# Ten output stores cut into 64, 49 and 15 rows, to share the rows unevenly among the DMA engines

## The chip, the core and the metric

The kernel runs on one NeuronCore of a Trainium2 chip. The metric is device time in microseconds, the median of several executions. A verdict of faster or slower needs 2%; the ratios come with a 95% interval.

## The reference

Grouped attention with four query positions, and its gradients:

```
B, Hq, Hkv, Sq, Sk, D = 32, 32, 4, 4, 2048, 128      # bf16
scores = einsum("bhqd,bhkd->bhqk", q, repeat(k, 8)) * D ** -0.5
out    = einsum("bhqk,bhkd->bhqd", softmax(scores), repeat(v, 8))
# returned: out, and the gradients of q, k, v for a given grad_out
```

K and V (with q and grad_out) are read once, and dK and dV (with out and dq) written once: 136.3 MB each way. There is little arithmetic for each byte.

## The kernel before

The host code lays K and V out as two arrays each, so that one batch is four loads and four stores of 128 rows with 8,192 or 8,448 bytes in a row (the longer rows carry q, grad_out, out and dq as well). Twenty buffers ("slots") hold loaded and finished rows. A precomputed string, `PLAN`, gives the order of all units of work and the slot of each; `emit` turns it into instructions. Every load and store is issued by SyncE, in the order of the plan.

```python
SLOTS, E_TILES, DS_TILES = 20, 2, 2
...
        if name in ("LK", "LV"):                      # load 128 rows into a slot
            x = slots[int(u.where, 36)]
            ...
            nc.sync.dma_start(out=x[:, 0:n], in_=src)
...
        elif name in ("DVe", "DKe"):                  # PSUM to the output slot
            i, g = divmod(i, 2)
            copy = nc.scalar.copy if u.where == "A" else nc.vector.tensor_copy
            copy(out=t[name[:2], "out", g][:, 2 * QW * i:2 * QW * i + 2 * QW], in_=t[name[:2], i, g])
        elif name in ("SV", "SK"):                    # store a slot
            half, g = divmod(i, 2)
            n = LONG if g else ROW
            w = (slice(0, n), slice(0, ROW // 2), slice(ROW // 2, n))[half]
            nc.sync.dma_start(out=(dv_r if name == "SV" else dk_r)[g][b][:, w], in_=t["D" + name[1], "out", g][:, w])
```

In the built program the DMA issues take eight semaphores in turn. From the ninth on, an issue waits until the DMA eight places before it has landed, so at most eight DMAs are in flight.

## Time and profile before

| | before |
|---|---|
| median | 677.4 us |
| data moved | 272.65 MB |
| DMA data queue busy, share of 16 engines | 98.4% |
| PE, ACT, DVE busy | 92%, 85%, 83% |

The table of windows of the kernel before follows. Each row is a stretch of 100 us: its length, busy us of PE, PE weight loads, DVE, ACT and GpSimd with counts, the granted clock, the busy share of the DMA engines, and GB/s.

```profile
core 0: us, PE busy (x) PEld busy (x) DVE busy (x) ACT busy (x) POOL busy (x), PEclk, DMA share, GB/s
...
100.00:200.00 100.00, 97.42 (x1399) 64.74 (x1399) 89.56 (x115) 92.90 (x135) 7.18 (x18) 1.00 1.01 422
200.00:300.00 100.00, 94.75 (x1418) 63.60 (x1417) 87.91 (x111) 89.89 (x131) 5.98 (x15) 1.00 1.01 424
300.00:400.00 100.00, 91.36 (x1308) 61.71 (x1296) 83.33 (x104) 85.50 (x124) 4.78 (x12) 0.97 1.01 414
400.00:500.00 100.00, 91.05 (x1322) 61.87 (x1320) 82.79 (x106) 84.94 (x124) 5.99 (x15) 0.97 1.01 411
500.00:600.00 100.00, 91.08 (x1292) 61.16 (x1294) 84.82 (x109) 88.60 (x128) 6.20 (x16) 1.00 1.01 405
```

The DMA engines look busy all the time, yet the rate falls after 300 us. The first five lines of the waits of SyncE's queue of DMA issues tell what an issue waited for (line, releaser, us in total, times, longest). L229 is the loads, L324 the stores.

```profile
SPq L229 <- DMA out_dram<-row: 226.4, 46, 8.2
SPq L324 <- DVE row L319: 79.3, 19, 14.9
SPq L324 <- ACT row L319: 71.5, 37, 9.2
SPq L324 <- DMA out_dram<-row: 57.8, 33, 2.3
SPq L229 <- DMA row<-in_v_dram: 32.4, 16, 2.8
```

Issues wait mostly for older DMAs to land. The landings of one DMA can be told apart: the trace has the semaphore updates, and a whole DMA makes 16, one for each DMA engine. Sorted, and counted back from the last one, they read as follows (medians over the whole transfers around each time):

```
us from start    first landing   8th     15th    16th (last)
100                 -3.2         -2.8    -0.2     0
200                 -6.2         -4.3    -0.4     0
300                -10.0         -5.4    -2.5     0
400                -10.6         -7.8    -4.5     0
```

The engines drift apart, because each works through its own share at its own pace. A DMA is complete only when the slowest has landed. From 300 us on the spread stays near 11 us: the fast engines now keep pace with the slowest. This is where the rate falls.

### The profile page before, as it was taken

To read this page: it belongs to the slowest core of one execution; us is meant where nothing else is said; L and a number is where in the kernel's file an instruction comes from. 1 tells how busy PE (TensorE), PEld (TensorE's weight loads), DVE (VectorE), ACT (ScalarE), POOL (GpSimd) and SP (SyncE) were. 2 spreads that over 40 slices of the span, in tenths; PEclk is the share of its full clock that TensorE was granted. 3 is DMA by queue.
4 is the path that set the end of the run, shared out by engine and by line. 5 is a ranking of instruction groups with operands and counts; after the bars stand their busy time and mean duration, and the time that the engine had idled before them with its cause. 6 is when DMAs were issued, how large, how long until landed. Compare 5 with 4: busy or idle time off the path is not lost.

```text
span 677.2 us, 20820 instructions
## 1 busy us (share of the span) xinstructions
PE 620.9 (92%) x8788; PEld 416.3 (61%) x8788; DVE 560.2 (83%) x712; ACT 578.8 (85%) x826; POOL 39.0 (6%) x102
## 2 busy tenths in 40 slices
PE   8899999999999999889999899989899889988995
PEld 7565666666666665656656565666666556655652
DVE  3678988989888888888878888879788888887886
ACT  5878999999999998888888889879888888997876
POOL 0000000000000000000000000000000000000000
PEclk9997999999999999999989999989989999998988
DMA  9999999999999999999999999999999999999698
GB/s 368 399 418 403 389 424 420 415 424 425 425 422 426 422 424 425 424 423 408 423 414 403 414 403 416 413 419 397 418 404 416 414 395 405 398 390 388 219 421 327
DMA packets 37533, 273.97 MB, mean 405 GB/s; under 512 B 4160, under 2 KB 4160, under 8 KB 5184
## 3 DMA queue, kind: packets, MB, share of 16 engines
q1 hardware_dynamic: 37440, 272.65, 98.4%
q8 instruction: 69, 1.13, 0.6%
q14 instruction: 24, 0.20, 0.1%
HBM read 136.31 MB, written 136.31 MB: 403 GB/s over the span
## 4 chain that ended last, share of the span: by engine, by line
DMA 61%; PE 25%; ACT 7%; DVE 3%; issue 2%; SPq 1%; DVEq 0%; ACTq 0%
DMA out_dram<-row 49%; PE psum L244 14%; DMA row<-in_k_dram 10%; ACT row L319 5%; PE psum L313 5%; PE psum L291 3%; PE psum L258 3%; DMA row<-in_v_dram 2%; SPq L229 1%; DVE row L319 1%; ACT vt_sb L212 1%; DVE vt_sb L214 1%; DVE dt_sb L214 1%; ACT kt_sb L212 0%; DVE e_sb L263 0%
## 5 line engine op out<-in xcount | busy, mean ns | idle before, releaser
L319 ACT CAST row<-psum 128x1024 bf16<-128x1024 f32 x302 | 297.3, 1026 | 46.7 <-PE psum L313 23.5
L244 PE MATMUL psum<-ident,row 128*128 128x128 f32 x2048 | 300.0, 286 | 19.8 <-DVE vt_sb L214 5.0
L319 DVE CAST row<-psum 128x1024 bf16<-128x1024 f32 x210 | 252.7, 1217 | 41.6 <-PE psum L313 20.6
L244 PEld LDWEIGHTS psum<-ident,row 128*128 128x128 f32 x2048 | 226.9, 144 | 94.4 <-ACT row L319 30.5
L212 ACT COPY kt_sb<-psum 128x512 f32<-128x512 f32 x181 | 106.0, 596 | 22.4 <-PE psum L244 18.2
L212 ACT COPY vt_sb<-psum 128x512 f32<-128x512 f32 x181 | 102.4, 605 | 8.6 <-PE psum L244 8.5
L306 DVE SCALAR_TENSOR_TENSOR ds_sb<-psum,delta,e_sb 128x1024 bf16<-128x1024 f32 x64 | 81.9, 1279 | 25.5 <-PE psum L258 24.6
L313 PE MATMUL psum<-e_sb,dop_sb 32*128 32x512 bf16 x512 | 79.0, 389 | 19.5 <-ACT row L319 18.8
L313 PE MATMUL psum<-ds_sb,qp_sb 32*128 32x512 bf16 x512 | 80.5, 390 | 4.5 <-DVE row L319 1.7
L263 DVE TENSOR_SCALAR_CACHE_REDUCE e_sb<-psum 128x2048 bf16<-128x2048 f32 x32 | 73.3, 2291 | 11.1 <-PE psum L258 11.0
L267 ACT ACTIVATE e_sb<-psum,m 128x2048 bf16<-128x2048 f32 x32 | 63.9, 1998 | 0.7 <-DVE e_sb L263 0.7
L214 DVE COPY kt_sb<-psum 128x1024 bf16<-128x1024 bf16 x75 | 51.0, 682 | 11.1 <-PE psum L244 10.5
L313 PEld LDWEIGHTS <-dop_sb 32*128 32x128 bf16 x512 | 24.3, 92 | 52.5 <-issue 44.7
L214 DVE COPY vt_sb<-psum 128x1024 bf16<-128x1024 bf16 x75 | 49.0, 683 | 5.0 <-PE psum L244 4.7
L274 POOL TENSOR_SCALAR dop_sb<-row,rinv 128x128 bf16<-128x128 bf16 x32 | 19.4, 605 | 576.9 <-DVE rinv L271 435.8
L313 PEld LDWEIGHTS <-qp_sb 32*128 32x128 bf16 x512 | 21.6, 91 | 46.6 <-issue 43.2
L291 PE MATMUL psum<-row,dt_sb 128*32 128x128 bf16 x2048 | 41.0, 222 | 0.3 <-DVE row L319 0.3
L291 PEld LDWEIGHTS <-dt_sb 128*32 128x32 bf16 x2048 | 33.4, 96 | 12.7 <-issue 7.9
L244 PE MATMUL psum<-ident,ds_sb 128*128 128x128 f32 x256 | 40.2, 281 | 1.0 <-ACT row L319 1.0
L258 PE MATMUL psum<-vt_sb,qdt_sb 128*32 128x512 bf16 x512 | 39.8, 385 | 0.9
L291 PEld LDWEIGHTS <-et_sb 128*32 128x32 bf16 x2048 | 30.7, 96 | 11.0 <-ACT et_sb L212 8.8
L258 PEld LDWEIGHTS <-qdt_sb 128*32 128x32 bf16 x1024 | 21.7, 95 | 25.1 <-issue 17.0
(34 smaller groups left out, 351.3 us busy)
## 6 DMA issues: line engine op xcount, KB each, us to landing
row<-in_k_dram SPq DMA_DIRECT2D x64, 1056.0 KB, 17.5
row<-in_v_dram SPq DMA_DIRECT2D x64, 1024.0 KB, 15.5
out_dram<-row SPq DMA_DIRECT2D x62, 1056.0 KB, 19.4
out_dram<-row SPq DMA_DIRECT2D x62, 1024.0 KB, 20.0
out_dram<-row SPq DMA_DIRECT2D x6, 512.0 KB, 4.4
out_dram<-row SPq DMA_DIRECT2D x2, 544.0 KB, 4.6
```

What stands on the lines that cost most here:

```text
L212: nc.scalar.copy(out=out.bitcast(FP32), in_=in_)
L214: nc.vector.tensor_copy(out=out, in_=in_.bitcast(BF16))
L229: nc.sync.dma_start(out=x[:, 0:n], in_=src)
L244: nc.tensor.transpose(out=ps[:, P * j:P * j + P], in_=src[:, 4 * half + j, :], identity=ident32[:])
L258: nc.tensor.matmul(out[r, QW * w:QW * w + QW], lhsT=t["qdt"][:, P * side + 32 * h:P * side + 32 * h + 32], rhs=t[x, NH * i + h][:, QW * w: ...
L263: nc.vector.tensor_scalar(out=t["e"][:], in0=t["S"], scalar1=-scale, scalar2=None, op0=ALU.mult, op1=ALU.min, accum_out=t["m"][:])
L267: nc.scalar.activation(out=t["e"][:], in_=t["S"], func=ACT.Exp, bias=t["m"][:], scale=scale, accum_out=t["l"][:])
L274: nc.gpsimd.tensor_scalar(out=t["dop"][:], in0=t["go"], scalar1=t["rinv"][:], scalar2=None, op0=ALU.mult)
L291: nc.tensor.matmul(t[name][r, :], lhsT=left[:, j, r, odd], rhs=right[:, 4 * i + j, :, odd], start=(i == 0 and c == 0), stop=(i == 1 and c ...
L306: nc.vector.scalar_tensor_tensor(out=t["ds"][:, w], in0=t["DP", i], scalar=t["dl"][:], in1=t["e"][:, w], op0=ALU.subtract, op1=ALU.mult)
L313: nc.tensor.matmul(acc[:, QW * (h % 2):QW * (h % 2) + QW], lhsT=t[still][rows[h], :], rhs=t[moving][rows[h], QW * i:QW * i + QW], start=Tr ...
L319: copy(out=t[name[:2], "out", g][:, 2 * QW * i:2 * QW * i + 2 * QW], in_=t[name[:2], i, g])
```

## The change

The intent is to move rows from engines that fall behind to engines that run ahead. In batches 1, 4, 7, ... the first dV store goes out as three DMAs of 64, 49 and 15 rows, which use 16, 7 and 15 engines. The plan was made anew for it: the whole `PLAN` string differs and is cut here.

```diff
+PARTS = slice(0, 64), slice(64, 113), slice(113, 128)
+
...
-    "a000e400e011f4A0f0A0e522f5D0e133f1A0a110c000d0A0e214f2D0e345f3A0e726f7D0e607f6A0i040i1-0b120g600g211h6A0h2A0g322"
+    "a000e400e511f4A0e122f1A0e033f0A0f5D0a110c000e644f6A0e215f2D0e326e737d0A0f7D0f3A0i040i1-0D0b120g200h2A0g311h3A0"
... (the rest of PLAN)
-            nc.sync.dma_start(out=(dv_r if name == "SV" else dk_r)[g][b][:, w], in_=t["D" + name[1], "out", g][:, w])
+            dst, src = (dv_r if name == "SV" else dk_r)[g][b][:, w], t["D" + name[1], "out", g][:, w]
+            for p in PARTS if name == "SV" and i == 0 and b % 3 == 1 else (slice(0, P),):
+                nc.sync.dma_start(out=dst[p], in_=src[p])
```

The condition holds in ten batches. The last batch, no. 31, stores by halves of the columns under other part numbers and is never split by rows.

## The prediction

> **What bounds it now.** The DMA engines. By the table of DMA queues the data queue is busy 98.4% of 16 engines' span; PE is 92% busy. Yet the rate falls: by the table of windows 422 to 424 GB/s at 100 to 300 us, 414, 411 and 405 in the next three hundreds. The waits of the DMA-issuing queue name stores: loads (L229) wait 226.4 us for `out_dram<-row`: a load needs a slot that a store has left on all 16 engines.
>
> The trace's semaphore updates tell why. Each DMA counts 16 landings, one per engine. Sorted, they split into seven early, eight middle, one late, and drift apart: first to last 3 us at 100 us, 7.8 at 254, 11 at 307. Then the spread stays at 10 to 11: all slots wait for the late engine, and the early engines starve. Between 150 and 300 us the interval between full DMAs is 2.49 us for the early ranks, 2.54 for the middle, 2.57 for the last; between 350 and 580 us it is 2.62 for all. So starving costs more than the late engine's own pace. Instruction fetches (69 packets of 16 KB, about 0.95 us each) are part of the unevenness.
>
> **What the change does.** The Trainium skill, "DMA: Bandwidth & Descriptors", section on why a DMA increments its semaphore by 16, says that such a DMA uses the largest divisor of its rows up to 16, on the lowest-numbered engines; its section on latency calls engines 7 and 15 usually slower. Then a split store gives engines 0-6 4+7+1=12 rows, 7-14 4+1=5, 15 4, instead of 8 each. The 7/8/1 grouping of the landings agrees; that no. 15 is the late one the trace doesn't tell (engines aren't named). A row of 8 KB takes 309 ns. In 11 batches (1, 4, ... 31): +13.6 us for seven engines, -10.2 for eight, -13.6 for one. Bytes stay. Added: 22 issues of about 0.35 us on a queue that mostly waits, and 242 semaphore packets of 9 ns.
>
> **Worth.** Per batch of eight DMAs (estimate from the intervals): early 19.91+0.41=20.32 us, middle 20.32-0.31=20.01, late 20.55-0.41=20.14. The slowest is now 20.3, where the kernel ran 20.5 until 300 us and 20.9 after. All of it is critical. 256 full DMAs at 2.54 = 650; plus start, 9 us (90 landed by 240 us); plus end, 4; plus stalls of the new plan. Before, the dip at 600 to 640 us (310 GB/s; the queue waits 16.4 us for L299 with loads behind it) cost about 10. I allow 3 us. PE's 19.4 us a batch leaves it 95% busy: little slack.
>
> Predicted: 666 us, 658 to 675. Faster by over 2% 0.36, within 2% 0.61, slower 0.03.
>
> **Signs.** Data queue: same 272.65 MB, 37,682 packets. Spread of the landings under 6 us at 300 us, no saturation near 11. Windows from 300 to 600 us at 418 GB/s or more. Loads' wait for stores well under 226 us; stores land in under 19.4 us. Early ranks no longer early: the middle eight lead by up to 12 us at the end.
>
> **What would make it wrong.** Engines 0-6 read 49 rows that other engines otherwise read: if rows collide in SBUF, 309 ns grows (seven rows, 11 times: 24 us if doubled). The middle group runs ahead until slots bind again. The compute chain, with PE at 95%, binds before DMA does. The new end has a dip of its own.

## The result, and the profile after

The changed kernel takes 708.4 us (707.1 to 709.5, four runs), against 677.7 us for the kernel before in the same rounds. The ratio is 1.0455, interval 1.0428 to 1.0482: slower by 4.5%. A ratio here is the mean time of one kernel's runs over that of the other's of the same rounds, so not quite the ratio of the medians quoted. Executions over 1.5% slower than the fastest of the same kernel are left out of the means.

The table of windows of the kernel after, same columns:

```profile
core 0: us, PE busy (x) PEld busy (x) DVE busy (x) ACT busy (x) POOL busy (x), PEclk, DMA share, GB/s
...
100.00:200.00 100.00, 91.41 (x1280) 61.41 (x1278) 83.88 (x110) 85.44 (x120) 4.79 (x12) 0.98 1.01 415
200.00:300.00 100.00, 91.70 (x1331) 61.85 (x1334) 83.39 (x110) 84.48 (x119) 5.98 (x15) 0.95 1.00 406
300.00:400.00 100.00, 88.85 (x1230) 59.80 (x1223) 79.36 (x103) 79.01 (x112) 5.98 (x15) 0.93 0.97 379
400.00:500.00 100.00, 90.56 (x1231) 60.14 (x1230) 80.14 (x104) 81.43 (x114) 4.79 (x12) 0.90 0.99 388
500.00:600.00 100.00, 86.93 (x1231) 58.64 (x1231) 79.09 (x103) 79.31 (x111) 5.98 (x15) 0.95 0.99 380
```

The rate was meant to stay at 418 GB/s or more after 300 us. It is 379 to 388, and the fall begins 100 us earlier. The low rate from 500 us on may in part be a dip that comes with the new order of units: e1_plan_only, an experiment below with that order and whole stores, has a lower rate there and still takes only 679.2 us.

```profile
500.00:600.00 100.00, 90.16 (x1240) 59.31 (x1239) 79.63 (x105) 81.31 (x115) 6.00 (x15) 0.93 0.93 366
```

The waits of SyncE's queue after (L231 loads, L328 stores):

```profile
SPq L231 <- DMA out_dram<-row: 176.9, 54, 5.5
SPq L328 <- DVE row L321: 100.4, 31, 10.8
SPq L231 <- DMA row<-in_v_dram: 64.7, 33, 2.8
SPq L328 <- DMA out_dram<-row: 64.6, 35, 3.2
SPq L328 <- ACT row L321: 36.8, 15, 6.6
```

The wait of loads for stores went down, from 226.4 to 176.9 us, as predicted, and the kernel is slower all the same. Loads wait more for V loads instead (64.7 us, 32.4 before), which no slot explains: these are waits for one of the eight semaphores. But both shifts come with the new order of units and not with the split, since e1_plan_only shows them too:

```profile
SPq L231 <- DMA out_dram<-row: 172.5, 44, 5.5
SPq L231 <- DMA row<-in_v_dram: 79.7, 41, 2.1
```

So these waits don't explain the loss, and a smaller total in one row of them is not a gain.

The data queue, before and then after (packets, MB, busy share):

```profile
q1 hardware_dynamic: 37440, 272.65, 98.4%
```

```profile
q1 hardware_dynamic: 37660, 272.65, 96.9%
```

Each engine that takes part in a DMA posts one semaphore packet. The three pieces together make 16+7+15=38 instead of 16, so 22 more, ten times: 220, and 37,660 is exactly that. The engine counts of the diff's intent are right. The Trainium skill, "DMA: Bandwidth & Descriptors", section "Why a DMA increments its semaphore by 16 and not by 1", gives the rule behind them (the largest divisor of the row count up to 16) and says that the issuing sequencer adds what is missing to 16 itself. The trace agrees on that too: a 49-row piece has eight updates, seven landings and one at the time of its issue.

The spread of the landings after, in the same form as before:

```
us from start    first landing   8th     15th    16th (last)
100                 -5.4         -3.2    -0.3     0
200                -13.5        -11.5    -5.8     0
300                -12.8        -12.0   -10.4     0
400                -14.7        -14.6   -13.2     0
```

It grows about twice as fast, and in the end fifteen engines stand close together, with one alone 10 to 13 us behind. The pieces of a single split store say which kind of engine that is. These are the landings of the ones issued at 366.1, 368.3 and 370.9 us, in us before the last landing of each:

```
64 rows, last landing 387.2:  -14.5 -14.3 -14.3 -14.2 -14.0 -13.8 -13.7 -13.4 -13.3 -13.2 -13.0 -12.7 -12.7 -12.7 -12.2  0
49 rows, last landing 389.5:  -14.6 -14.5 -14.4 -13.9 -13.9 -13.2   0
15 rows, last landing 389.8:  -16.2 -16.2 -15.7 -15.4 -15.0 -15.0 -15.0 -14.6 -14.5 -14.4 -14.4 -13.9 -13.9 -13.2   0
```

The late engine is one of the seven that take the 49 rows. It gets 4+7+1=12 rows of a split store instead of 8. The change loads the engine that it was to relieve.

### The profile page after: what moved, and what is told of

Read it like the earlier page. It is cut to its first block, busy times and chain, and to the rows that moved or that the text cites. A ratio compares the mean times of both kernels' runs of the same rounds, so it can differ in the third digit from the quotient of the medians.

```text
span 705.2 us, 20835 instructions
## 1 busy us (share of the span) xinstructions
PE 629.6 (89%) x8788; PEld 420.8 (60%) x8788; DVE 565.7 (80%) x734; ACT 576.8 (82%) x804; POOL 39.1 (6%) x102
## 3 DMA queue, kind: packets, MB, share of 16 engines
q1 hardware_dynamic: 37660, 272.65, 96.9%
## 4 chain that ended last, share of the span: by engine, by line
DMA 56%; PE 29%; ACT 6%; DVE 4%; issue 3%; SPq 0%; ACTq 0%; DVEq 0%
DMA out_dram<-row 30%; DMA row<-in_v_dram 22%; PE psum L246 17%; PE psum L315 6%; ACT row L321 5%; DMA row<-in_k_dram 5%; PE psum L260 3%; PE psum L293 3%; DVE row L321 1%; DVE dt_sb L216 1%; DVE vt_sb L216 1%; DVE ds_sb L308 1%; DVE e_sb L265 0%; ACT e_sb L269 0%; SPq L231 0%
## 5 line engine op out<-in xcount | busy, mean ns | idle before, releaser
L321 ACT CAST row<-psum 128x1024 bf16<-128x1024 f32 x324 | 319.7, 1024 | 73.0 <-DMA out_dram<-row 43.5
L246 PEld LDWEIGHTS psum<-ident,row 128*128 128x128 f32 x2048 | 234.3, 147 | 83.3 <-ACT row L321 38.0
L321 DVE CAST row<-psum 128x1024 bf16<-128x1024 f32 x188 | 228.5, 1219 | 46.1 <-DMA out_dram<-row 39.8
L214 ACT COPY kt_sb<-psum 128x512 f32<-128x512 f32 x183 | 106.3, 597 | 16.2 <-PE psum L246 15.7
L315 PE MATMUL psum<-e_sb,dop_sb 32*128 32x512 bf16 x512 | 84.3, 412 | 35.0 <-ACT row L321 34.9
L216 DVE COPY vt_sb<-psum 128x1024 bf16<-128x1024 bf16 x124 | 82.4, 685 | 15.8 <-PE psum L246 14.2
L214 ACT COPY vt_sb<-psum 128x512 f32<-128x512 f32 x132 | 74.9, 597 | 10.5 <-PE psum L246 10.3
L315 PEld LDWEIGHTS <-dop_sb 32*128 32x128 bf16 x512 | 21.8, 92 | 65.2 <-issue 54.6
L260 PE MATMUL psum<-vt_sb,qdt_sb 128*32 128x512 bf16 x512 | 43.1, 414 | 1.0 <-ACT row L321 0.4
L260 PE MATMUL psum<-kt_sb,qdt_sb 128*32 128x512 bf16 x512 | 35.1, 382 | 3.9 <-DVE row L321 3.7
```

The lines of the kernel that those rows point to most:

```text
L214: nc.scalar.copy(out=out.bitcast(FP32), in_=in_)
L216: nc.vector.tensor_copy(out=out, in_=in_.bitcast(BF16))
L246: nc.tensor.transpose(out=ps[:, P * j:P * j + P], in_=src[:, 4 * half + j, :], identity=ident32[:])
L260: nc.tensor.matmul(out[r, QW * w:QW * w + QW], lhsT=t["qdt"][:, P * side + 32 * h:P * side + 32 * h + 32], rhs=t[x, NH * i + h][:, QW * w: ...
L315: nc.tensor.matmul(acc[:, QW * (h % 2):QW * (h % 2) + QW], lhsT=t[still][rows[h], :], rhs=t[moving][rows[h], QW * i:QW * i + QW], start=Tr ...
```

## The experiments

Three theories were tested. A: the rows of the one late engine set the time, and the split gives it more. B: the pieces cost the time as such, because each takes one of eight semaphores. C: the new order of units is worse by itself. "The late engine" is written as no. 4 where the probe below is presupposed.

### The parts alone, and a split that moves no rows

e1_plan_only is the changed kernel with whole stores; e2_split_only is the kernel before with the split; e3_three_even is the changed kernel with three pieces that leave every engine its eight rows.

```diff
 # e1_plan_only, against the changed kernel
-PARTS = slice(0, 64), slice(64, 113), slice(113, 128)
+PARTS = slice(0, 128),
 # e3_three_even, against the changed kernel
-PARTS = slice(0, 64), slice(64, 113), slice(113, 128)
+PARTS = slice(0, 48), slice(48, 96), slice(96, 128)
 # e2_split_only, against the kernel before: PARTS and the loop over it as in the change, PLAN untouched
```

> The new order of units, every store whole. Theory A (one engine that is already late is among the seven that take the 49 rows, so the split gives it 12 rows instead of 8) and theory B (the split takes three of the eight DMA semaphores, so less work is in flight) both put the loss into the split: 668 to 682 us, first-to-last spread of landings as before, saturating near 10 to 11 us. Theory C (the new order of units is worse by itself): 700 us or more.

> The old order of units, with the split in the same ten stores. A and B: 695 to 715 us, with the spread of landings saturating near 13 us well before 250 us, and the rate below 400 GB/s after it. C: within 1% of 677.7 us.

> The new order, the same ten stores in three pieces of 48, 48 and 32 rows: each engine gets 3+3+2=8 rows as in a whole store, but three semaphores are taken as in the change. A: as e1_plan_only within 1%. B: as the changed kernel, 700 us or more. If both act, in between.

| kernel | order | pieces | rows of the late engine | median us | ratio to before (interval) |
|---|---|---|---|---|---|
| before | old | whole | 8 | 677.5 | 1 |
| e1_plan_only | new | whole | 8 | 679.2 | 1.0015 (0.9987 to 1.0043) |
| e3_three_even | new | 48, 48, 32 | 8 | 682.8 | 1.0063 (1.0025 to 1.0101) |
| e2_split_only | old | 64, 49, 15 | 12 | 693.2 | 1.0220 (1.0189 to 1.0252) |
| changed kernel | new | 64, 49, 15 | 12 | 708.4 | 1.0455 (1.0428 to 1.0482) |

C falls: the new order alone costs nothing that is clear of noise. B explains about 3.6 us, the difference of e3_three_even and e1_plan_only; their intervals overlap, so that it is hardly clear of noise itself. Moving the rows costs the rest, some 25 us in the new order. In the old order the split costs 15.7 us: 693.2 us is just below the 695 to 715 expected. The spread of landings in e2_split_only reached 11 us at 200 us instead of 300, but stayed at 11 to 12 where 13 was expected, and its rate was 401 to 411 GB/s between 100 and 500 us and 389 only after that, where less than 400 was expected. The spread in e1_plan_only missed too: it went on to 13 us at 400 us instead of 10 to 11, but the 15th landing came only 7.8 us before the last there, against 13.2 in the changed kernel.

### Which engine is late

The section of the skill quoted above says that a DMA issued by SyncE runs on the lowest-numbered engines. If so, pieces of 1, 2, 3, ... rows ask one more engine each time.

```diff
 # e4_probe, against the kernel before
+PIECES = {10: (1, 2, 3, 4, 5, 6, 7, 100), 13: (8, 9, 10, 11, 12, 13, 14, 51), 16: (15, 98, 15)}
-            nc.sync.dma_start(out=(dv_r if name == "SV" else dk_r)[g][b][:, w], in_=t["D" + name[1], "out", g][:, w])
+            dst, src = (dv_r if name == "SV" else dk_r)[g][b][:, w], t["D" + name[1], "out", g][:, w]
+            at = 0
+            for n in PIECES.get(b, (P,)) if name == "SV" and i == 0 else (P,):
+                nc.sync.dma_start(out=dst[at:at + n], in_=src[at:at + n])
+                at += n
```

> The old order; the first dV store of batch 10 goes in pieces of 1, 2, 3, 4, 5, 6, 7 and 100 rows, that of batch 13 in 8 to 14 and 51 rows, that of batch 16 in 15, 98 and 15. If a piece of n rows uses the n lowest engines, the landings of the pieces name each engine's lag. The prediction's reading (the late engine is no. 15): no piece below 16 engines lands with the late one; every piece lands 3 to 9 us before the whole store beside it. Theory A: from some n below 8 on, the last landing of a piece comes with the late landing of the whole stores, 4 us or more after its other landings. The time itself may be 1 to 2% longer by the many pieces.

Landing times in us from the start, of the load just before the pieces and of the first five pieces in batch 10:

```
whole:    242.2 242.3 242.3 242.5 243.1 244.5 245.7 245.8 246.3 246.4 246.7 247.1 247.5 247.9 248.9 251.1
1 row :   242.6
2 rows:   242.9 244.8
3 rows:   243.2 243.4 245.1
4 rows:   243.5 243.7 245.4 246.1
5 rows:   244.6 244.7 245.7 246.4 251.4
```

No piece on up to four engines lands with the late engine. The first on five engines does: 251.4 us, just after the whole load's 251.1. So the fifth engine is the late one, no. 4 if the numbering of the skill holds. The four before it are not alike either; the second and the fourth are some 2 and 3 us behind the first. The groups of seven, eight and one of the prediction were real as counts, but they are not runs of engine numbers. The single run took 685.1 us, against the 677.5 us median of before, so 1.1% longer, as expected for the added pieces.

The skill's section "Latency and other measured facts" calls engines 7 and 15 usually slower, with a guess that puts it down to DMAs issued by GpSimd. The prediction left that guess out. No DMA of this kernel is issued by GpSimd, and the late engine is the fifth; in batch 16 the first piece of 15 rows lands at 390.8 us, right after the whole load's 390.4, so that the late engine is not no. 15 there either.

### One row more for the fifth engine

Two splits with equally many pieces, in all 31 batches before the last. The first leaves the fifth engine its 8 rows, the second gives it 9. The other early-numbered engines, 0 to 3, get 9 rows in both.

```diff
 # against the kernel before, with the loop of e4_probe over PIECES in every batch
+PIECES = 64, 60, 4      # e6_four: 16, 15 and 4 engines
+PIECES = 48, 75, 5      # e7_five: 16, 15 and 5 engines
```

> The old order; the first dV store of all 31 batches before the last goes as 64, 60 and 4 rows: by the divisor rule engines 0-3 get 4+4+1=9 rows, 4-14 get 8, no. 15 gets 4. The probe says that the late engine is the fifth, no. 4: its rows stay at 8. Theory A: only the cost of 62 more issues and taken semaphores, estimated from e3_three_even against e1_plan_only (3.6 us for 20 more) at up to 11 us: 678 to 689 us. If the late engine were among the first four: 9 us more than e7_five's other engines would allow, no difference to e7_five.

> As e6_four, with 48, 75 and 5 rows: engines 0-4 get 3+5+1=9, 5-14 get 8, no. 15 gets 3. As many pieces; what differs for the rows is that no. 4 gets 9 instead of 8, 31 times: 31 x 0.31 = 9.6 us. Theory A: 8 to 13 us longer than e6_four. If the loss comes from uneven pieces or from semaphores and not from the rows of no. 4: equal to e6_four within 3 us.

e6_four took 695.1 us (median of its three fast runs; ratio 1.0257, 1.0224 to 1.0289), e7_five 704.8 us (1.0399, 1.0363 to 1.0435). The difference, 9.7 us, is inside the expected 8 to 13 and close to 31 rows of 0.31 us. But the landings don't bear out theory A here. In e7_five the piece of five rows lands before the piece of 75 in 27 of the 31 split stores, by 0.2 to 3.6 us. So the engine that finishes such a store last is none of the first five; it is one of nos. 5 to 14, which have their 8 rows. Why e7_five is slower than e6_four is therefore open, and the agreement in size may be luck. The split stores of the next section are the cleaner test.

The packets confirm the engine counts again. First e6_four, 19 more for each of 31 stores; then e7_five, 20 more:

```profile
q1 hardware_dynamic: 38029, 272.65, 98.7%
```

```profile
q1 hardware_dynamic: 38060, 272.65, 98.2%
```

What missed is the cost of e6_four itself. It is 17 us slower than before, where at most 11 were expected. That would be 0.27 us for each of 62 added issues, against 0.18 us in e3_three_even (3.6 us for 20). It is not the price of the pieces alone: in 16 of the 31 split stores the piece of four rows lands last of all, so that there one of engines 0 to 3, with their ninth row, is the late one. The waits for places in flight did grow. The two largest that no slot explains wait for loads:

```profile
SPq L231 <- DMA row<-in_k_dram: 88.2, 38, 3.2
SPq L329 <- DMA row<-in_v_dram: 86.5, 40, 3.0
```

From the trace's issues and landings, all eight places in flight are taken 93% of the time between 200 and 300 us in e6_four, 41% in the kernel before. A piece of four rows takes a place like a whole store. But that this fullness makes up the cost is not shown. Between 100 and 600 us every DMA of e6_four but the pieces of four rows had been issued 7 us or more before the one ahead of it landed, so that the engine that lands last never ran out of work.

### The changed kernel with the weight elsewhere, and doses

Three more splits of the same ten stores: one uneven as the change is but sparing the fifth engine, in both orders, and one between.

```diff
 # e8_four_new against the changed kernel; e9_four_old the same against e2_split_only
-PARTS = slice(0, 64), slice(64, 113), slice(113, 128)
+PARTS = slice(0, 64), slice(64, 124), slice(124, 128)
 # e11_ten_rows against the changed kernel
-PARTS = slice(0, 64), slice(64, 113), slice(113, 128)
+PARTS = slice(0, 32), slice(32, 107), slice(107, 128)
```

> The changed kernel with its ten split stores as 64, 60 and 4 rows instead of 64, 49 and 15: the same count of pieces, also uneven, but no. 4 gets 8 rows instead of 12. Theory A: as e3_three_even, 679 to 687 us. If uneven pieces as such, or rows read by another engine than usual, cost the time: 695 us or more.

> The old order with the ten split stores of e2_split_only as 64, 60 and 4 rows: no. 4 keeps 8 rows. Theory A, whose direct cost is 10 x 4 rows x 0.317 = 12.7 us: e2_split_only (693.2) less 12.7, so 678 to 683 us. If it stays at 690 us or more, the pieces cost the time in the old order, not the rows of no. 4.

> The changed kernel with the ten stores as 32, 75 and 21 rows: no. 4 (and 0-6) get 2+5+3=10 rows, between e8_four_new's 8 (684.1 us) and the change's 12 (708.4 us). If the loss is in proportion to the rows of no. 4 with the doubled slope that these two runs show: 696 us, 693 to 700. If only the direct cost of rows acts (3.2 us a row) and the rest of the 24 us comes from something else in the 64/49/15 split: 688 to 692 us.

| rows of the fifth engine in a split store | old order | new order |
|---|---|---|
| 8 | e9_four_old 680.8 us | e8_four_new 684.1 us |
| 10 | | e11_ten_rows 693.2 us |
| 12 | e2_split_only 693.2 us | changed kernel 708.4 us |

The same number of pieces, also uneven, gives 24.3 us back in the new order once the fifth engine is spared. Rows read by another engine than usual are therefore not the main trouble. In the old order the difference is 12.4 us, and 10 x 4 rows x 0.317 = 12.7 us were expected from the rows alone. The landings agree here: in all ten split stores of e9_four_old the piece of four rows lands 0.7 to 9.4 us before the piece of 60, so that the late engine is not one of nos. 0 to 3. In this pair the fifth engine's rows are paid for almost one for one. Engines 5 and 6 get as many rows as the fifth in both runs; that it is the fifth alone rests on the probe.

In the new order two rows cost 9.1 us and the next two 15.2, more than the 6.3 us that 20 rows take. e11_ten_rows fell at the lower end of the range of the proportional reading (693 to 700) and just above the other (688 to 692); the cost bends upward, which neither reading had. Part of it can be placed. The steps from one last landing to the next add up to the run, so the 22.5 us by which the profiled runs of the changed kernel and e8_four_new differ can be divided among the kinds of DMA (without the pieces of four rows, which no. 4 takes no part in). The pieces of a split store take 1.41, 2.43 and 0.31 us in the mean, 4.15 in sum, against 2.81 for the two pieces of e8_four_new: 13.4 us in all. K loads take 5.0 us more, all of it in the seven that follow a split store directly (3.25 us each, against 2.55), and the stores of the long rows 4.8 us more (2.80 us each, against 2.72). In e2_split_only, the old order, only one K load follows a split store directly; it takes 3.87 us. The late engine never ran out of work in this: between 100 and 600 us every DMA had been issued 11 us or more before the one ahead of it landed (5 us or more in the kernel before). So its rows took longer. Why they do so is open.

### More in flight, by way of GpSimd

```diff
 # e5_more_in_flight, against the kernel before
-            nc.sync.dma_start(out=...)
+            (nc.gpsimd if name == "SK" and i == 0 else nc.sync).dma_start(out=...)
```

> The old order, all stores whole; the first dK store of 31 batches is issued by GpSimd, whose DMAs have semaphores of their own, so up to nine or more DMAs can be in flight instead of eight. If the eight semaphores are what lets the late engine starve the others (interval 2.62 us after 330 us against its own pace of 2.57): 668 to 674 us. If slots and the order of units set it, or GpSimd's issue costs something: 675 us or more. The spread of landings may then grow beyond 11 us.

It took 684.7 us, ratio 1.0101 (1.0074 to 1.0128). It didn't do what it was made for. By the trace the DMAs in flight never exceeded eight and were fewer on average, 6.1 between 200 and 300 us against 7.2. The loads now wait long for PE, because stores that no longer stand in SyncE's queue no longer hold them back to the time for which the plan had placed them:

```profile
SPq L229 <- PE psum L313: 136.1, 23, 11.4
SPq L229 <- PE psum L291: 71.6, 14, 12.1
```

That reading is argued from these lines. The run settles nothing on the eight semaphores.

No version that beats both kernels came out. If a DMA from SyncE always starts at the lowest engine, as the skill has it, a smaller DMA can spare the fifth engine only by going to engines 0 to 3. No split that gives the fifth engine fewer than 8 rows was tried.

## Why the prediction was wrong

- **"What bounds it now": right, with one wrong clause.** The rate falls when the fast engines can run no further ahead, and loads wait for stores. But "starving costs more than the late engine's own pace" doesn't hold as put. The late engine always had work queued, and its own row time is what the kernel pays for, as e2_split_only and e9_four_old show by 12.4 us for 40 rows. The interval of 2.62 us after 350 us is the late engine's own, slower than its 2.57 before. The prediction didn't look where it loses the time: in the stores. In the kernel before, between 100 and 600 us, the last landing follows the one ahead by a median 2.54 us for a K load and 2.45 for a V load, but by 2.80 and 2.58 us for the stores of as many bytes. As an estimate that is 0.8 us for each batch of eight DMAs, 24 us over 31 batches. What slows its stores is not known.
- **"The 7/8/1 grouping of the landings agrees": this is the step that failed.** Sorted landings give counts, not engine numbers. The counts 7, 8 and 1 matched those of the split, and were taken for engines 0-6, 7-14 and 15. The match was luck. The prediction even said "that no. 15 is the late one the trace doesn't tell", and then booked -13.6 us for it. The probe shows that the late engine is the fifth. It received four rows more in each split store, 12.7 us of its time in ten stores, instead of four fewer. The 64, 49 and 15 rows themselves went to 16, 7 and 15 engines as predicted.
- **"Worth: early 20.32, middle 20.01, late 20.14" fell with it.** The direct sum has the opposite sign for the late engine: 20.55 + 0.41 = 20.96 us a batch. That alone would make 13 us over the run, which the old order shows (693.2 against 680.8 us). The new order doubles it.
- **"In 11 batches (1, 4, ... 31)": ten.** Batch 31 stores by halves, so 37,660 packets and not 37,682.
- **"22 issues of about 0.35 us on a queue that mostly waits": the cost was looked for in the wrong place.** The time of the issue is hidden, but each piece takes one of eight places in flight. What that costs stays small or open: about 0.18 us a piece in e3_three_even, hardly clear of noise. The prediction never mentions the eight semaphores, though loads landed a median 15.5 to 17.5 us after their issue and stores 19 to 20, which is six to eight DMAs of 2.5 us.
- **"I allow 3 us" for the new plan: about right alone** (e1_plan_only, 1.7 us), and wrong together with the split.
- **"What would make it wrong" named collisions in SBUF, PE and a dip at the end.** A late engine that the split doesn't relieve was not listed. It is what happened. e8_four_new argues against collisions as the main cause; the dip was there (e1_plan_only, 366 GB/s from 500 to 600 us), but that run was no slower than before.
- **Loads' wait for stores "well under 226 us": it came true** (176.9 us), but by the new order: e1_plan_only has 172.5 us.

## What to carry to other kernels

A DMA is done when its slowest engine is done, so where DMAs bound a kernel and the engines drift apart, the rows of one engine can be worth their full time (12.4 us for 40 rows here). Before moving work among engines, find out which one is late: a single store cut into pieces for 1, 2, 3, ... engines names it in one run. Look again after rows have been moved: in e7_five the last engine was another one. Sorted landings that fall into groups of the right size are no evidence of which engines stand in them. Count what each extra DMA takes besides issue time, here one of eight semaphores.

## What the Trainium skill lacked or had wrong

- "DMA: Bandwidth & Descriptors", "Latency and other measured facts": it names engines 7 and 15 as usually slower, with a guess that concerns DMAs issued by GpSimd alone. Here, with none of these in the program, an engine is late all the same, the fifth of the lowest-first order: 251.4 us where the first four land by 246.1.
- The same page says nothing of how far engines may drift apart under a steady load: first to last landing 3 us at 100 us and 11 us after 300 us in the kernel before, up to 15 us in the changed one; or that one engine's extra rows can be paid nearly in full (12.4 us for 40 rows), or that an engine can be late in stores and not in loads (2.80 us for a store, 2.54 for a load of as many bytes).
- The same page, "Rules for kernel authors", advises against two transfers to disjoint halves of the partitions, since they serialize. The pieces of the changed kernel do land one after the other (387.2, 389.5 and 389.8 us), and e3_three_even puts a price of about 0.18 us, hardly clear of noise, on an added piece. No page tells of the eight semaphores that bound what is in flight in this program.
- The same page, "Why a DMA increments its semaphore by 16 and not by 1", was right in all that was checked: engine counts 16, 15, 7, 5 and 4 by packets (37,660, 38,029 and 38,060), and one further update at the issue of a smaller DMA. That the lowest-numbered engines are taken is in line with the probe, where each larger piece repeats the lags of the smaller ones; no trace here shows the numbers.
